# Weight pieces of an mLSTM cell with a gated projection: two blocks at a time, on two DMA queues

## The chip, the core and the metric

The kernel runs on one core of a Trainium2 chip. The core has five engines with an instruction queue each: TensorE (PE in the profile, with its weight loads as PEld), VectorE (DVE), ScalarE (ACT), GpSimd (POOL) and SyncE (SP), which only issues transfers here. Every engine works through its own instructions in the order in which the program wrote them. Sixteen DMA engines move data between HBM and the on-chip memory of 128 partitions; transfers that SP issues stand in the queue that the profile calls q1, those that GpSimd issues in q0. The metric is the device time of one execution in microseconds (us); a kernel's time is the median of several runs.

## The reference

Two parts follow each other. The first is an mLSTM cell over 4 batches, 8 heads, 768 steps and head dimension 40:

```python
m_new = np.maximum(f_gate[:, :, t] + m, i_gate[:, :, t])
f_stab = np.exp(f_gate[:, :, t] + m - m_new)
i_stab = np.exp(i_gate[:, :, t] - m_new)
C = f_stab[:, :, None, None] * C + i_stab[:, :, None, None] * np.einsum('bhd,bhe->bhde', vt, kt)
n = f_stab[:, :, None] * n + i_stab[:, :, None] * kt
h_tilde = np.einsum('bhde,bhe->bhd', C, qt)
denom = np.maximum(np.abs(np.einsum('bhd,bhd->bh', n, qt)[:, :, None]), 1.0)
y[:, :, t] = o * h_tilde / denom          # o: sigmoid of o_gate
```

Its result, as 3072 tokens of 320 features, goes through a gated projection:

```python
g = x @ w_gate                            # 320 x 1536
silu = g * (1.0 / (1.0 + np.exp(-g)))
val = x @ w_val                           # 320 x 1536
return (silu * val @ w_out).astype(np.float32)   # 1536 x 320
```

The three weight matrices are float64 in HBM; all else is float32.

## The kernel before

The 768 steps are cut into 6 groups of 128 (two chunks of 64 each). A group goes through the cell as matrix products (scores of q and k, weighted by a table w_sb, plus what comes from the state C), is turned into xT, and then through the projection. The first group is done in a special way while inputs and weights are still on their way; from the second on all weights lie on the chip, and the projection uses a scheme with fewer products (`gated`, `project_seven`). The order of work is written out by hand, since the kernel asks for a manual schedule.

**Weights in pieces.** The 1536 columns of w_gate and w_val make 12 blocks of 128 columns; a block's gate half goes to partitions 0 to 63 and its value half to partitions 64 to 127, 320 KB each as float64. w_out makes three pieces of four blocks over all 128 partitions. `PIECES` (L162) lists the transfers: before the change blocks 0 to 5 as pieces 0 to 5 of one block, blocks 6 to 11 as pieces 6 to 8 of two blocks, w_out as pieces 9 to 11. `piece_load(p, home, parts)` (L166) issues one piece: a gate transfer (part 0) and two value transfers (parts 1 and 2, the first with four fifths of the bytes). Gate halves go by SP and value halves by GpSimd, except that pieces 2 to 5 go by GpSimd altogether (L200). The raw words land in one of two rotating buffers of the pool tile `raw`, in the tail of h_sb (blocks 2 and 3, a place in which q and k of the first group lie densely before), or in wo_sb (piece 7).

**Conversion.** A block is turned to float32 in four steps: `scale` (L221) with two ScalarE instructions (top, L226, and low, L228), `join` (L231) with two VectorE instructions (L235, L236), and `rounded` (L240) with one addition on GpSimd, or on VectorE for some blocks (L243). There is one top buffer and two low buffers, so blocks are converted one after the other.

**The first group's loop.** `hidden(0, m)` (L740) runs for m = 0 to 11. TensorE multiplies block m (20 matmuls, L748); then the loop converts an older block that `ahead` (L1011) names (block 3 at m = 1, block 4 at m = 2, to block 11 at m = 9); then ScalarE applies silu (L753) and VectorE multiplies (L754) to fill h_sb. So the conversion's instructions stand ahead of the silu on ScalarE, and of the product on VectorE. Two blocks' products fit into the four PSUM banks, so block m + 2 waits for block m's silu and product. Behind each block `slots[m]` (L1012) puts other work:

- 0: pieces 6 and 7 are asked for. 1: `late_sums`, a scan on VectorE. 2: `late_maxima`, the store of M_sb to DRAM by GpSimd, and the load of k for the next group by SP.
- 3: `late_decay`, then on SP the load of w_sb (M_sb read back, spread over partitions), of q and of v.
- 4: an exp, some small tables, and piece 8 (blocks 10 and 11). 5: transposes and decays. 6: transposes of k, `weights_cap` (L530, VectorE on w_sb), piece 9.
- 7: `weights_sub` (L519, VectorE), `weights_exp` (L537, ScalarE), `weigh_values` (L395, GpSimd, with v).
- 8: a memset of q_sb, the scores (L384), piece 10, the load of o_gate. Before these, in the middle of block 8's matmuls, q is transposed (L351) and copied to qT by ScalarE.

After the loop, `project_all` multiplies with w_out, and the groups 1 to 5 follow.

**Ahead of the loop** (L642 to L708) stands the first group's cell work. There SP gets the gates of pieces 0 and 1, GpSimd their values, and then, behind `first_gate(1, ...)` (L692), GpSimd gets pieces 2 to 5 (L693).

SP's and GpSimd's transfers each stand in the order of issue, and an engine that issues can be held at a transfer: SP when the queue is behind, GpSimd when the eighth transfer before has not landed.

Of the kernel before, what the change touches and what calls it, by code (L numbers as in the profile page):

```python
# [12 lines left out]
U32 = mybir.dt.uint32  # L13
AF = mybir.ActivationFunctionType
# [10 lines left out]
def kernel(  # L25
# [18 lines left out]
    nc = tc.nc  # L44
# [9 lines left out]
    NFC = DF // 128  # L54
# [3 lines left out]
    NKC = DM // HP  # L58
    UH = BH // 2
    UA = UH // 2  # L60
    NH = NFC + 1
# [15 lines left out]
    def bank(name, tag="cell"):  # L77
        return psum.tile([128, 512], F32, name=name, tag=tag)
# [41 lines left out]
    wo_sb = const.tile([128, NFC, DM], F32)  # L120
    h_sb = const.tile([128, NH, TW], F32)
# [37 lines left out]


    raws = {}
    PIECES = [("gv", m, 1) for m in range(NFC // 2)] + [("gv", m, 2) for m in range(NFC // 2, NFC, 2)] + [("o", m, 4) for m in range(0, NFC, 4)]  # L162

    homes = {}

    def piece_load(p, home=None, parts=(0, 1, 2)):  # L166
        kind, m, n = PIECES[p]
        if kind == "gv":
            a, d = NKC, n * 128
            gate_w, val_w = (w[:, m * 128:(m + n) * 128].rearrange("(c p) f -> p c f", p=HP) for w in (moe_w_gate, moe_w_val))  # L170
            src = [(slice(0, HP), slice(0, NKC), gate_w), (slice(HP, 128), slice(0, NKC - 1), val_w[:, 1:]),
                   (slice(HP, 128), slice(NKC - 1, NKC), val_w[:, 0:1])]
        else:
            a, d = n, DM
            src = [(slice(0, 128), slice(0, n), moe_w_out[m * 128:(m + n) * 128].rearrange("(a p) d -> p a d", p=128))]
        if src[0][2].dtype == F32:
            for r, cs, w in [src[x] for x in parts if x < len(src)]:
                if kind == "o":
                    nc.sync.dma_start(out=wo_sb[r, m:m + n, :], in_=w)
                else:  # L180
                    for x in range(n):
                        nc.sync.dma_start(out=wgv_sb[r, m + x, cs], in_=w[:, :, ts(x, 128)])
            return
        if p in homes:
            raw = homes[p]
        else:
            if p < 6:
                if p in (0, 4):
                    homes["raw"] = conv.tile([128, 4 * NKC * 128], U32, name="raw")
                base = h_sb[:, NH - NKC:].rearrange("p m t -> p (m t)").bitcast(U32) if p in (2, 3) else homes["raw"]  # L190
                raw = base[:, ds(2 * a * d if p in (1, 3, 5) else 0, 2 * a * d)]
            elif home is None:
                raw = conv.tile([128, 4 * NKC * 128], U32, name="raw")
            else:
                raw = home.rearrange("p a t -> p (a t)").bitcast(U32)
            raw = homes[p] = raw[:, 0:2 * a * d]
        for x in parts:
            if x < len(src):
                r, cs, w = src[x]
                eng = nc.gpsimd if x or 1 < p < 6 else nc.sync  # L200
                eng.dma_start(out=raw[r].rearrange("p (a d) -> p a d", a=a)[:, cs], in_=w.bitcast(U32))
        words = raw.rearrange("p (a d two) -> p a d two", two=2, a=a)
        raws[p] = (words[:, :, :, 0], words[:, :, :, 1])
        split(p)
# [16 lines left out]
    def scale(j):  # L221
        if j in blocks:
            lo, hi, dst = blocks[j]
            a, d = hi.shape[1], hi.shape[2]
            top = conv.tile([128, NKC * 128], F32, name="top", bufs=1).rearrange("p (a d) -> p a d", a=a)
            nc.scalar.mul(top, hi.bitcast(F32), 2.0 ** -112)  # L226
            low = conv.tile([128, NKC * 128], I32, name="low").rearrange("p (a d) -> p a d", a=a)
            nc.scalar.mul(low, lo, 2.0 ** -29)  # L228
            blocks[j] = (low, top.bitcast(U32), dst)
# [81 lines left out]
    step1 = keep1  # L311
# [250 lines left out]
    A, V, G = nc.scalar, nc.vector, nc.gpsimd  # L562
# [63 lines left out]
    def first_gate(P, engs, pad):  # L626
        for u, eng in zip((2 * P, 2 * P + 1), engs):
            x = x_sb[:, u, 0:DM].rearrange("p (h d) -> p h d", d=D)
            eng.tensor_tensor(x, x, o_sb[:, u * H:(u + 1) * H], op=ALU.mult)
        copy(pad, x_sb[:, 2 * P:2 * P + 2, DM:], x_sb[:, 2 * P:2 * P + 2, 0:HP])  # L630
# [12 lines left out]
        copy(eng, state(2)[:, P * UA:(P + 1) * UA], ps)  # L643

    GATE, VALUE = (0,), (1, 2)
    burn(7, "gen")
    for f in (first_mask, first_inputs, first_maxima):
        for x in range(B):
# [19 lines left out]
    for p in range(2):  # L668
        piece_load(p, parts=GATE)
    turn_one(1, q_sb, qT, (V, A))  # L670
    first_values(0)
    piece_load(0, parts=VALUE)
    first_own(0)
    turn_one(1, k_sb, kT, (A, A))
# [15 lines left out]
    first_x(3)  # L690
    seam(0, 0, (A, A, A, A))
    first_gate(1, (G, V), V)  # L692
    for p in range(2, 6):  # L693
        piece_load(p)
    scale(0)
    ps0 = first_state(0, "gen")
    seam(0, 1, (V, A, A, A))
# [312 lines left out]
    on_vector = (9, 10, 11)  # L1010
    ahead = {0: [], 1: [3], 2: [4], 3: [5], 4: [6], 5: [7], 6: [8], 7: [9], 8: [10], 9: [11], 10: [], 11: []}  # L1011
    slots = {  # L1012
        0: [run(piece_load, 6), run(piece_load, 7, wo_sb)],
        1: [run(late_sums)],
        2: [run(late_maxima), run(M_store, G), run(load_all, k_sb, k, 1)],
        3: [run(late_decay), run(weights_load, 1), run(load_all, q_sb, q, 1), run(load_all, v_sb, v, 1)],
        4: [run(nc.scalar.activation, step1, step1, AF.Exp), run(decay_rows), run(cap_table), run(piece_load, 8)],
        5: [run(late_turns), run(decay)],
        6: [run(turn_one, P, k_sb, kT, (A, A)) for P in range(2)] + [run(weights_cap, 0), run(weights_cap, 1), run(piece_load, 9)],
        7: [run(weights_sub, 1, 0), run(weights_sub, 1, 1), run(weights_exp, 0), run(weights_exp, 1), run(weigh_values, G, 0),  # L1020
            run(weigh_values, G, 1)],
        8: [run(nc.gpsimd.memset, q_sb, 0.0), run(do_scores), run(piece_load, 10), run(load_all, o_sb, o_gate, 1)],
        9: [run(do_weigh, 0), run(do_weigh, 1), run(do_decayed, 2)],
        10: [run(do_add, 1, (0,)), run(rounded, 12), run(load_squares, q_sq, q, 2, (0,))],
        11: [run(do_intra, 0), run(do_inter, 1, 0), run(do_gather, 1, 0, False), run(piece_load, 11),
             run(load_squares, q_sq, q, 2, (1,))],
    }
    amid = {8: [run(turn_one, P, q_sb, qT, (A, A)) for P in range(2)], 11: [run(do_add, 1, (1,)), run(do_state, 2)]}
# [122 lines left out]
```

## Time and profile before

| | |
|---|---|
| Median of 3 runs | 516.66 us (516.08 to 516.69) |
| The profiled execution, its own time | 515.42 us |
| Its span, first to last instruction | 513.5 us |
| PE busy, PEld busy | 98%, 83% of the span |
| DVE, ACT, POOL busy | 65%, 41%, 52% |
| Granted TensorE clock | 1.00 |
| HBM read, written | 35.68 MB, 4.01 MB |
| DMA queue q1 (SP) | 36.95 MB, 45.4% of 16 engines |
| DMA queue q0 (GpSimd) | 5.33 MB, 4.7% of 16 engines |

A group of instructions is shown with its line, engine, operation and tiles (out<-in); times are from the start of the span. A timeline row has the start, the length, the engine, the line, the operation, the tiles and the count, and in square brackets the engine's idle time before it with what ended it. SP's rows show how long SP was held at an issue. The DMA share of a stage is the mean busy share of the 16 engines; it can be above 1 where packets overlap. A matmul's end is modelled, so busy PE is not PE at its peak.

### The profile page before, as it was taken

How to read it: one execution, taken by the hardware profiler on the slowest of the kernel's cores; microseconds unless marked ns; L12 is line 12 of the kernel's file. 1: busy time of each engine (PE TensorE's matmuls, PEld its weight loads, DVE VectorE, ACT ScalarE, POOL GpSimd, SP SyncE). 2: the span in 40 equal slices, each digit the busy share in tenths (PEclk: the TensorE clock that was granted, in tenths of full speed). 3: DMA queues.
4: the chain of work that ended last, by engine and by line, in shares of the span. 5: the costliest groups of instructions: out<-in, count | busy, mean ns of one | idle time of the engine just before them, and what ended most of it. 6: DMA issues, size and time to landing. Idle time of an engine off the chain costs nothing.

```text
span 513.5 us, 15092 instructions
## 1 busy us (share of the span) xinstructions
PE 502.5 (98%) x6437; PEld 424.9 (83%) x6437; DVE 332.7 (65%) x543; ACT 208.1 (41%) x404; POOL 264.6 (52%) x296
## 2 busy tenths in 40 slices
PE   8999979999899999999999999999999999999996
PEld 4855545667788899888899888899988899988896
DVE  5889557688897777588467578558558554233421
ACT  3684746448343339321338321338321340223200
POOL 3773442366689663367652357651447650166710
PEclk9999999999999999999999999999999999999999
DMA  9999997798621992501992501992101200000001
GB/s 148 189 213 223 182 180 211 154 156 103 96 46 28 166 124 39 91 4 26 163 129 39 88 8 20 165 130 40 42 3 17 39 2 27 27 1 0 1 14 38
DMA packets 184154, 43.29 MB, mean 84 GB/s; under 512 B 173048, under 2 KB 179592, under 8 KB 183448
## 3 DMA queue, kind: packets, MB, share of 16 engines
q1 hardware_dynamic: 182276, 36.95, 45.4%
q0 software_dynamic: 1680, 5.33, 4.7%
q8 instruction: 50, 0.82, 0.7%
q14 instruction: 16, 0.13, 0.1%
q10 hardware_dynamic: 132, 0.07, 0.0%
HBM read 35.68 MB, written 4.01 MB: 77 GB/s over the span
## 4 chain that ended last, share of the span: by engine, by line
PE 84%; DMA 4%; ACT 4%; DVE 3%; POOL 2%; issue 1%; SPq 1%; DVEq 0%; POOLq 0%
PE gv_x L898 24%; PE o_ps L819 22%; PE gv_y L898 20%; PE gv_ps L748 5%; PE o_ps L765 3%; PE inter L433 2%; DMA w_sb<-M_dram 2%; PE intra L442 2%; PE sp L384 2%; ACT w_sb L534 2%; DMA M_dram<-M_sb 1%; PE add L410 1%; ACT h_sb L583 1%; SPq L368 1%; PE sp L600 1%
## 5 line engine op out<-in xcount | busy, mean ns | idle before, releaser
L898 PE MATMUL gv_x<-xT,wgv_sb 64*128 64x256 f32 x720 | 89.1, 377 | 0.0
L898 PEld LDWEIGHTS gv_x<-xT,wgv_sb 64*128 64x128 f32 x720 | 69.3, 187 | 8.1 <-issue 0.2
L819 PE MATMUL o_ps<-wo_sb,h_sb 128*128 128x160 f32 x480 | 67.4, 300 | 0.0
L819 PEld LDWEIGHTS o_ps<-wo_sb,h_sb 128*128 128x128 f32 x480 | 65.6, 190 | 1.7 <-issue 1.7
L946 ACT ACTIVATE h_sb<-gv_x 128x256 f32<-128x256 f32 x30 | 11.5, 383 | 115.7 <-PE gv_x L898 115.7
L748 PE MATMUL gv_ps<-xT,wgv_sb 64*128 64x512 f32 x240 | 54.3, 596 | 0.1
L748 PEld LDWEIGHTS gv_ps<-xT,wgv_sb 64*128 64x128 f32 x240 | 25.4, 187 | 23.9 <-issue 20.2
L898 PE MATMUL gv_y<-xT,wgv_sb 64*128 64x256 f32 x360 | 43.9, 376 | 0.0
L898 PE MATMUL gv_y<-q_sb,wgv_sb 64*128 64x256 f32 x360 | 43.9, 376 | 0.0
L395 POOL TENSOR_TENSOR vw_sb<-v_sb,w_sb 128x656 f32<-128x656 f32 x10 | 13.8, 1376 | 52.3 <-ACT w_sb L534 40.5
L898 PEld LDWEIGHTS gv_y<-xT,wgv_sb 64*128 64x128 f32 x360 | 34.9, 187 | 4.0
L898 PEld LDWEIGHTS gv_y<-q_sb,wgv_sb 64*128 64x128 f32 x360 | 34.9, 187 | 4.0
L819 PE MATMUL o_ps<-wT,S 128*128 128x160 f32 x240 | 33.4, 299 | 0.0
L819 PEld LDWEIGHTS o_ps<-wT,S 128*128 128x128 f32 x240 | 32.9, 190 | 0.0
L898 PE MATMUL gv_x<-q_sb,sw 64*128 64x256 f32 x240 | 31.0, 377 | 1.2 <-POOL sw L872 1.2
L534 ACT ACTIVATE w_sb<-w_sb,g_T 128x64 f32<-128x64 f32 x128 | 31.0, 334 | 0.0
L919 POOL TENSOR_TENSOR h_sb<-x_sb 128x512 f32<-128x512 f32 x12 | 15.8, 1313 | 24.6 <-ACT x_sb L918 24.6
L939 POOL TENSOR_TENSOR tmp<-tmp 128x512 f32<-128x512 f32 x15 | 20.2, 1344 | 14.9 <-DVE tmp L938 14.9
L919 POOL TENSOR_TENSOR h_sb<-tmp 128x512 f32<-128x512 f32 x13 | 16.5, 1271 | 21.5 <-ACT tmp L918 21.5
L786 POOL TENSOR_TENSOR S<-h_sb 128x256 f32<-128x256 f32 x30 | 22.7, 756 | 9.4 <-DVE h_sb L919 7.4
L765 PE MATMUL o_ps<-wo_sb,h_sb 128*128 128x320 f32 x96 | 27.2, 438 | 0.0
L898 PE MATMUL gv_y<-q_sb,sw 64*128 64x256 f32 x200 | 27.0, 388 | 0.2 <-DVE tmp L916 0.2
(226 smaller groups left out, 988.3 us busy)
## 6 DMA issues: line engine op xcount, KB each, us to landing
w_sb<-M_dram SPq DMA_DIRECT2D x10, 512.0 KB, 6.7
v_sb<-in_v_dram SPq DMA_DIRECT2D x12, 320.0 KB, 5.8
o_sb<-in_o_gate_dram SPq DMA_DIRECT2D x12, 320.0 KB, 5.6
raw<-in_moe_w_out_dram SPq DMA_DIRECT2D x3, 1280.0 KB, 6.8
k_sb<-in_k_dram SPq DMA_DIRECT2D x10, 320.0 KB, 7.7
x_sq<-k_sb SPq DMA_DIRECT2D x64, 40.0 KB, 3.0
q_sb<-in_q_dram SPq DMA_DIRECT2D x32, 64.0 KB, 3.3
out_dram<-tmp SPq DMA_DIRECT2D x24, 80.0 KB, 1.7
```

Source lines behind the costliest of these rows:

```text
L384: nc.tensor.matmul(sp[two][half(i), a, :], lhsT=kT[feats(two), P * UA + a, half(i)], rhs=qT[feats(two), P * UA + a, half(i)], start=True, ...
L395: eng.tensor_tensor(vw_sb[:, heads(P)], v_sb[:, heads(P)], w_sb[:, heads(P), last].to_broadcast([128, UH, D1]), op=ALU.mult)
L433: nc.tensor.matmul(inter[two][half(i), a, :], lhsT=qT[feats(two), P * UA + a, half(i)], rhs=state(2 * n + i)[feats(two), P * UA + a, :], s ...
L534: nc.scalar.activation(w_sb[:, h], w_sb[:, h], AF.Exp, bias=g_T[:, n, h:h + 1], scale=-1.0)
L748: nc.tensor.matmul(ps[i], lhsT=wgv_sb[half(i), m, kc, :], rhs=x[half(i), kc, :], start=(kc == 0), stop=(kc == NKC - 1))
L765: nc.tensor.matmul(ps[u], lhsT=hid(g, m)[:, ts(u, L)], rhs=wo_sb[:, m, :], start=(m == 0), stop=(m == NFC - 1))
L786: eng.tensor_tensor(S1[:, k], lo[:, second_half], hi[:, second_half], op=ALU.add)
L819: nc.tensor.matmul(node[x][:, i], lhsT=lhs(k)[:, ts(i, L)], rhs=rhs(k), start=start and k == 0 and i == 0, stop=stop and k == KH - 1, skip ...
L898: nc.tensor.matmul(ps[:, i, cols], lhsT=lhs(c)[half(i)], rhs=rhs(c)[half(i)], start=start and c == 0, stop=stop and c == n - 1, skip_group ...
L919: (nc.vector if k == KH - 1 else nc.gpsimd).tensor_tensor(h_sb[:, 2 * k + 1], uw[:, 0], uw[:, 1], op=ALU.mult)
L939: nc.gpsimd.tensor_tensor(uw[:, :, second_half], uw[:, :, second_half], uw[:, :, first_half], op=ALU.add)
L946: nc.scalar.activation(h[:, first_half], x[:, 0, first_half], AF.Silu)
```

## The change

Blocks 2 to 9 are listed as pieces of two blocks, so the list has 10 pieces instead of 12 and the later ones get new numbers: 2 (blocks 2 and 3), 3 (4 and 5), 4 (6 and 7), 5 (8 and 9), 6 (10 and 11), 7 to 9 (w_out). Every gate half now goes by SP and every value half by GpSimd. Piece 2 takes the whole tail of h_sb; a one-column memset by GpSimd (`raw_h`) stands in front of it, for which its transfers wait. Piece 3 takes the second `raw` buffer; the others land where the same blocks landed before. Pieces 2 and 3 are asked for where pieces 2 to 5 were. Piece 6 (blocks 10 and 11) is asked for in slot 5 instead of slot 4, and the load of v moves from slot 3 to slot 5, behind it. On SP the order becomes w_sb, q, gates of blocks 10 and 11, v; it was w_sb, q, v, gates of blocks 10 and 11. Nothing is computed in another way.

```diff
-    PIECES = [("gv", m, 1) for m in range(NFC // 2)] + [("gv", m, 2) for m in range(NFC // 2, NFC, 2)] + [("o", m, 4) for m in range(0, NFC, 4)]
+    PIECES = [("gv", 0, 1), ("gv", 1, 1)] + [("gv", m, 2) for m in range(2, NFC, 2)] + [("o", m, 4) for m in range(0, NFC, 4)]
...
-            if p < 6:
-                if p in (0, 4):
+            if p < 2:
+                if p == 0:
                     homes["raw"] = conv.tile([128, 4 * NKC * 128], U32, name="raw")
-                base = h_sb[:, NH - NKC:].rearrange("p m t -> p (m t)").bitcast(U32) if p in (2, 3) else homes["raw"]
-                raw = base[:, ds(2 * a * d if p in (1, 3, 5) else 0, 2 * a * d)]
+                raw = homes["raw"][:, ds(2 * p * a * d, 2 * a * d)]
...
-                eng = nc.gpsimd if x or 1 < p < 6 else nc.sync
+                eng = nc.gpsimd if x else nc.sync
...
+    raw_h = h_sb[:, NH - NKC:]
...
-    for p in range(2, 6):
-        piece_load(p)
+    nc.gpsimd.memset(raw_h[:, 0, 0:1], 0.0)
+    piece_load(2, raw_h)
+    piece_load(3)
...
-        0: [run(piece_load, 6), run(piece_load, 7, wo_sb)],
+        0: [run(piece_load, 4), run(piece_load, 5, wo_sb)],
...
-        3: [run(late_decay), run(weights_load, 1), run(load_all, q_sb, q, 1), run(load_all, v_sb, v, 1)],
-        4: [run(nc.scalar.activation, step1, step1, AF.Exp), run(decay_rows), run(cap_table), run(piece_load, 8)],
-        5: [run(late_turns), run(decay)],
+        3: [run(late_decay), run(weights_load, 1), run(load_all, q_sb, q, 1)],
+        4: [run(nc.scalar.activation, step1, step1, AF.Exp), run(decay_rows), run(cap_table)],
+        5: [run(piece_load, 6), run(load_all, v_sb, v, 1), run(late_turns), run(decay)],
```

In slots 6, 8 and 11 only the numbers of the w_out pieces change (9, 10, 11 to 7, 8, 9).

More of the change, by code (lines that the diff above doesn't have):

```diff
@@ L1012 @@
     slots = {
-        0: [run(piece_load, 6), run(piece_load, 7, wo_sb)],
+        0: [run(piece_load, 4), run(piece_load, 5, wo_sb)],
         1: [run(late_sums)],
         2: [run(late_maxima), run(M_store, G), run(load_all, k_sb, k, 1)],
-        3: [run(late_decay), run(weights_load, 1), run(load_all, q_sb, q, 1), run(load_all, v_sb, v, 1)],
-        4: [run(nc.scalar.activation, step1, step1, AF.Exp), run(decay_rows), run(cap_table), run(piece_load, 8)],
-        5: [run(late_turns), run(decay)],
-        6: [run(turn_one, P, k_sb, kT, (A, A)) for P in range(2)] + [run(weights_cap, 0), run(weights_cap, 1), run(piece_load, 9)],
+        3: [run(late_decay), run(weights_load, 1), run(load_all, q_sb, q, 1)],
+        4: [run(nc.scalar.activation, step1, step1, AF.Exp), run(decay_rows), run(cap_table)],
+        5: [run(piece_load, 6), run(load_all, v_sb, v, 1), run(late_turns), run(decay)],
+        6: [run(turn_one, P, k_sb, kT, (A, A)) for P in range(2)] + [run(weights_cap, 0), run(weights_cap, 1), run(piece_load, 7)],
         7: [run(weights_sub, 1, 0), run(weights_sub, 1, 1), run(weights_exp, 0), run(weights_exp, 1), run(weigh_values, G, 0),
             run(weigh_values, G, 1)],
-        8: [run(nc.gpsimd.memset, q_sb, 0.0), run(do_scores), run(piece_load, 10), run(load_all, o_sb, o_gate, 1)],
+        8: [run(nc.gpsimd.memset, q_sb, 0.0), run(do_scores), run(piece_load, 8), run(load_all, o_sb, o_gate, 1)],
         9: [run(do_weigh, 0), run(do_weigh, 1), run(do_decayed, 2)],
         10: [run(do_add, 1, (0,)), run(rounded, 12), run(load_squares, q_sq, q, 2, (0,))],
-        11: [run(do_intra, 0), run(do_inter, 1, 0), run(do_gather, 1, 0, False), run(piece_load, 11),
+        11: [run(do_intra, 0), run(do_inter, 1, 0), run(do_gather, 1, 0, False), run(piece_load, 9),
              run(load_squares, q_sq, q, 2, (1,))],
```

## The prediction

> **What bounds the kernel now.** I read the page first. TensorE's row is full, and a busy row may hide stalls, so I looked for the stretch in which the change works. The weight blocks come in the first 95 us, behind them the span is made of products that only follow in order. There I asked first for the DMA engines by stage (columns: stage and its length in us; busy time of PE, weight loads, DVE, ACT, POOL; granted clock, DMA share, GB/s):
>
> ```profile
> 26.00:33.00 7.00, 6.94 (x62) 3.94 (x60) 5.72 (x12) 6.55 (x13) 5.18 (x9) 1.00 1.04 218
> 37.00:41.00 4.00, 4.00 (x22) 2.14 (x20) 3.96 (x3) 1.84 (x3) 2.56 (x3) 1.00 1.04 200
> 41.00:44.00 3.00, 3.00 (x18) 1.56 (x16) 2.96 (x6) 0.23 (x1) 1.43 (x2) 1.00 1.05 300
> ...
> 84.00:86.00 2.00, 2.00 (x57) 1.00 (x54) 2.00 (x5) 0.60 (x1) 0.00 (x0) 1.00 1.03 412
> ```
>
> The DMA engines are busy throughout and yet move 218, 200, 300 or 412 GB/s. At 26 to 33 us all is GpSimd's queue, which brings one half of a block at a time to 64 partitions; at 84 to 86 us an output piece goes to 128 partitions; at 41 to 44 us SP brings gate halves (partitions 0 to 63) while GpSimd brings value halves (64 to 127). The queues of that last stretch:
>
> ```profile
> q0 software_dynamic: 167, 0.55, 62.6%
> q1 hardware_dynamic: 167, 0.33, 39.7%
> ```
>
> So GpSimd's queue moved 183 GB/s and SP's 110 beside each other. Next, who waits for weights on ScalarE, whose scaling (L226, L228) is the first of the conversion's steps:
>
> ```profile
> 31.01 0.80 ACT L226 ACTIVATE top<-h_sb 128x640 f32<-128x640 f32 x1 [0.39 <-DMA h_sb<-in_moe_w_val_dram]
> ...
> 34.12 0.80 ACT L226 ACTIVATE top<-h_sb 128x640 f32<-128x640 f32 x1 [1.15 <-DMA h_sb<-in_moe_w_val_dram]
> ...
> 37.17 0.80 ACT L226 ACTIVATE top<-raw 128x640 f32<-128x640 f32 x1 [0.23 <-DMA raw<-in_moe_w_val_dram]
> ...
> 44.51 0.79 ACT L226 ACTIVATE top<-raw 128x640 f32<-128x640 f32 x1 [3.27 <-DMA raw<-in_moe_w_val_dram]
> ...
> 48.72 0.79 ACT L226 ACTIVATE top<-raw 128x640 f32<-128x640 f32 x1 [2.25 <-DMA raw<-in_moe_w_val_dram]
> ```
>
> Blocks 2 to 6 arrive just in time or late for ScalarE. Did TensorE pay? Its timeline:
>
> ```profile
> 27.39 26.12 PE L748 MATMUL gv_ps<-xT,wgv_sb 64*128 64x512 f32 x120
> 53.44 0.80 PE L719 MATMUL tp_g<-x_sq 32*128 32x32 f32 x10
> ...
> 67.64 0.71 PE L351 MATMUL tp_kq<-x_sq,q_sb 64*128 64x64 f32 x16 [0.64 <-DMA q_sb<-in_q_dram]
> 69.98 0.71 PE L351 MATMUL tp_kq<-x_sq,q_sb 64*128 64x64 f32 x16 [1.63 <-DMA q_sb<-in_q_dram]
> ...
> 73.51 2.13 PE L384 MATMUL sp<-qT,kT 40*64 40x64 f32 x126 [0.16 <-ACT qT L143]
> ```
>
> Six blocks take 26.12 us, 4.35 each, and weight loads 0.43 apart make 4.3: hardly. The stall is later: q, then the scores, which wait for ScalarE's copies of qT. What holds these is on VectorE and SP:
>
> ```profile
> 63.95 2.36 DVE L530 TENSOR_TENSOR w_sb<-w_sb,cap 128x1024 f32<-128x1024 f32 x2 [3.52 <-DMA w_sb<-M_dram]
> ```
>
> ```profile
> 32.07 18.12 SPq L139 DMA_DIRECT2D k_sb<-in_k_dram  x1
> ```
>
> ```profile
> 53.42 1.13 SPq L515 DMA_DIRECT2D w_sb<-M_dram  x2
> 54.65 8.65 SPq L139 DMA_DIRECT2D q_sb<-in_q_dram  x2
> 63.40 5.97 SPq L139 DMA_DIRECT2D v_sb<-in_v_dram  x2
> 69.60 1.44 SPq L201 DMA_DIRECT2D raw<-in_moe_w_gate_dram  x1
> ```
>
> SP sat 18.12 us on the second half of k behind the backlog of weights. The chain of waits runs through M_sb's store (issued 46.17, 7.23 us) and w_sb's load (53.96, 9.87 us). Blocks 10 and 11 are asked for at 69.60 and wanted by ScalarE at 76.61.
>
> **The change, part by part.** *Issues.* GpSimd loses the 12 issues of blocks 2 to 5 (0.72, 0.63 and 0.56 us a block, 7.6 us) and gains 4 (2.4 us) and a memset of one column (0.15 by the nearest memset row). It also waited four times there, 2.8 us, for older DMAs. Its next work, the addition for block 3, starts at 37.57 and is needed at 40.4, so this is worth nothing. SP gains two issues of 0.60; it is idle from 22.0 to 30.0, so they are free. They wait for the memset (about 24.0, GpSimd's gating ends at 23.89). Behind them stand the gates of blocks 6 to 9 (which wait for block 1's scaling until 29.97 as before) and k, not wanted until 58.9. Blocks 10 and 11's values (1.17 us of GpSimd, 53.50) move behind the addition for block 7, into 2.33 us idle before that for block 8: free.
>
> *When blocks 2 and 3 are there.* This is the step that can cost. Before, each block was complete by itself: block 2 at 31.0, block 3 at 34.1. Now both come at once, in 640 KB of gate and 640 KB of value. The values need 0.655 MB / 183 GB/s = 3.6 us, the gates 0.655 / 110 = 6.0 us. From an issue at 24.1 and 0.9 us to the first packet they end at 31.0; landing follows some 2.1 us after, as an estimate from block 2 (0.655 MB at 218 behind what is left of block 1 ends near 28.8; there at 30.9). That is 33.1. Bounds: 31.5 when both queues share evenly at 300 GB/s (1.31 MB in 4.4 us), 37 when there is no overlap and blocks 4 and 5 mix in. I take 33.1, from the only stretch with gate and value side by side.
>
> *What 2.1 us later cost.* ScalarE's scaling of block 2 stands ahead of the silu of block 0, and VectorE follows: join, addition, product of block 0, join of block 3, product of block 1, then the scan of late_sums (37.58). VectorE's slack there is the 0.67 us that it waited for the silu of block 1; TensorE's is 1.2 (product of block 0 ends at 34.94, block 2's matmuls begin at 36.15). So 1.5 us passes on to late_sums, the join of block 4, M_sb and TensorE's blocks 4 and 5. Cost 1.5. Block 4 has 2.5 us of slack (37.17 against its join at 41.26, behind the scan), block 5 now comes with it; the waits of 3.27 and 2.25 go, and uncover only ScalarE's idle time.
>
> *What is gained behind it.* Blocks 2 to 9 are 5.24 MB. Two queues side by side (300 GB/s while values last, 200 for the gates left) end near 44.5 instead of 48.4, so k ends near 48.5 and M_sb's store, issued at 47.7, has the engines nearly to itself: landing at 51 (a small load took 2.3). Blocks 10 and 11's values no longer lie beside w_sb's load, whose median to landing is 6.7: w_sb at 57.7 where it was 63.9. VectorE wants it after the product of block 6, 59.75 + 0.69 + 1.3 = 61.7, so its idle 3.52 goes: gain 3.5. q, behind w_sb, lands by 65 even beside the moved values; TensorE wants it at 67.7: its idle 0.64 and 1.63 go, which lie inside the 3.5. What is late next is ScalarE: table load, exp (2.19) and qT copies, at 70.7 where they were at 72.40. All of that is 3.5 - 1.5 = 2.0. Then the gates of blocks 10 and 11, now in front of v: there by 69, wanted at 73. TensorE waited 0.75 where 0.24 is usual for block 8's silu, held by that scaling: gain 0.5. v, moved behind, lands near 71.5 as before; its user on GpSimd waits there already, and the products it feeds are at 83. SP's later issues wait for block 11's scaling, which moves forward too.
>
> Sum: -1.5 + 3.5 + 0.5 = 2.5 us less; beyond 95 us the order is unchanged and TensorE passes a shift on to the end. The profiled execution has a span of 513.5 and a time of 515.42, 1.24 under the median 516.66; taken off the median: **514.2 us**. Each us that block 2 comes later than 33.1 costs about 1.15 (VectorE's whole delay, and what TensorE had left); the gain is 0 at 35.3, and 1.03 lost (0.2%, about what a measurement can tell from no change) at 36.2.
>
> A rule that speaks against it: the Trainium skill, "SBUF — State Buffer", section "Can I just issue two DMAs to hit both halves?", says no: two DMAs on the two halves of the partitions gained 6% and serialize. By it the 218 GB/s would become 231 (an estimate from that page), blocks 2 and 3 with what goes between them would come at 35.6 to 38.4, and the sum would be 0.4 to 3.6 us lost, 517.0 to 520.2. The trace doesn't agree: the row at 41 to 44 us has 300, 38% more than 218.
>
> **Rivals.** *One: no price.* The queues share evenly; block 2 is there at 32.0, 1.3 us less is lost: gain 3.8, 512.9 us. For it: the row at 300. Against: 167 packets of each queue there, and GpSimd's are twice as large.
>
> *Two: SP's gates starve, the kernel gets slower.* Place: the landing of blocks 2 and 3 on ScalarE. In 37 to 41 us the sum was 200, and SP's gates issued at 30.0 took 12.6 us to land. If both halves of blocks 2 to 5 run as at 26 to 33 us, and values of blocks 4 and 5 go ahead of the first gates, 1.96 to 2.62 MB must pass at 218: 25.0 + 9.0 to 12.0 + 2.1 is 36.1 to 39.1. A third of the way, at 37.0, since some overlap is in the rows, the sum is 2.0 lost: 518.6 us. It decides from 36.2 on. Against: both halves of the mix at 37 to 41 went largely to the same partitions, and a GpSimd backlog of four DMAs stood before those gates; now there is one.
>
> *Three: the weights are hidden, nothing moves.* Block 2 at 34.4 to 36.2: the late gain pays the early loss, within 1 us: 516.5. For it: TensorE lost under 1 us to weights before 53 us.
>
> **How the numbers follow.** Forecast (2.5 less, block 2 between 32.3 and 34.4, 513.2 to 515.6): 0.45. Rival one 0.11, rival three 0.20, rival two 0.24. Faster is 0.45 + 0.11 = 0.56, same 0.20, slower 0.24. The range takes in rival one whole (no early loss at all, block 2 at 31.8 or before, is 4.0 less: 512.7) and rival two up to 36.6: 512.5 to 518.2. Left out is the worse half of rival two, 0.12.
>
> **What would show it.** ScalarE's first scaling that reads h_sb begins near 33.1 and the next one 2 to 3 us later with no DMA wait; the DMA rows of 25 to 38 us show near 300 GB/s; SP's 18 us on k end by 47; VectorE's cap (L529 there) has no wait for w_sb; TensorE's transposes of q have none for q; ScalarE's scaling near 72 has none for the gate weights. Wrong makes it: a first scaling after 35, GB/s near 220 with both queues on, or w_sb still waited for.

## The result, and the profile after

The changed kernel took 513.93 us (median of 20 runs, 512.51 to 517.04), the kernel before 516.48 us on the same chips (20 runs, 514.59 to 518.26). The ratio is 0.9959, with a 95% interval from 0.9945 to 0.9974: 2.1 us less (1.3 to 2.8), where 2.5 us were forecast. One of the twelve executions of a kernel further down (single blocks by two queues) and three of the twelve of another (the second with gates before w_sb) took more than 1.5% longer than their kernel's shortest, at a lower granted clock; medians and ratios leave them out. The profiled execution of the changed kernel took 514.3 us, with a span of 511.9.

The total came out near the forecast, in part by luck: the landing on which its largest cost rests was 1.8 us late and the cost larger than its term, and some of what made up for it was not in the sum. I follow the views in the order of the prediction. First the DMA engines by stage, in the changed kernel (columns as before: stage and length, busy time of PE, weight loads, DVE, ACT, POOL, granted clock, DMA share, GB/s):

```profile
26.00:29.00 3.00, 2.94 (x56) 2.21 (x53) 2.75 (x7) 2.97 (x7) 0.93 (x2) 1.00 0.92 206
29.00:32.00 3.00, 3.00 (x16) 1.34 (x12) 2.18 (x4) 2.03 (x5) 1.33 (x3) 1.00 1.02 218
32.00:43.00 11.00, 9.61 (x44) 5.40 (x44) 7.12 (x10) 5.69 (x9) 2.56 (x4) 1.00 1.05 298
```

From 32 us on, gates and values do run beside each other at 298 GB/s. In the six microseconds that decide about blocks 2 and 3 they don't: 206 and 218 GB/s, where GpSimd's halves alone had 218 before. The queues at 26 to 29 us, and then at 29 to 32 us, say why:

```profile
q1 hardware_dynamic: 274, 0.56, 84.0%
q0 software_dynamic: 20, 0.06, 8.5%
...
q0 software_dynamic: 138, 0.52, 81.1%
q1 hardware_dynamic: 75, 0.12, 20.0%
```

First SP's gates had the engines nearly to themselves, and then GpSimd's values. The gates of the first two-block piece, issued at 24.32, landed at 31.03; the values, issued at 24.59 and 25.25, landed at 33.95 and 34.64. So ScalarE's first scaling of that piece begins at 34.86, where I had put 33.1:

```profile
34.86 0.79 ACT L225 ACTIVATE top<-h_sb 128x640 f32<-128x640 f32 x1 [3.83 <-DMA h_sb<-in_moe_w_val_dram]
37.13 0.79 ACT L225 ACTIVATE top<-h_sb 128x640 f32<-128x640 f32 x1 [0.31 <-DVE wgv_sb L235]
```

TensorE pays for it between block 1 and block 2, and its row of blocks, unbroken before, now has a gap. The rest of its timeline in the changed kernel:

```profile
27.76 8.98 PE L749 MATMUL gv_ps<-xT,wgv_sb 64*128 64x512 f32 x40
38.14 17.94 PE L749 MATMUL gv_ps<-xT,wgv_sb 64*128 64x512 f32 x80 [1.40 <-DVE wgv_sb L242]
56.01 0.81 PE L720 MATMUL tp_g<-x_sq 32*128 32x32 f32 x10
...
69.40 1.16 PE L350 MATMUL tp_kq<-x_sq,q_sb 64*128 64x64 f32 x32
72.26 2.58 PE L383 MATMUL sp<-qT,kT 40*64 40x64 f32 x128
74.78 8.98 PE L749 MATMUL gv_ps<-xT,wgv_sb 64*128 64x512 f32 x40
84.45 1.14 PE L409 MATMUL add<-vw_sb,k_sb 64*64 64x41 f32 x62 [0.32 <-DVE w_sb L390]
```

The transposes after block 5 (tp_g) begin at 56.01 where they began at 53.44, 2.57 us later. The scores begin at 72.26, where two of the 128 matmuls began at 73.02 and the rest at 73.51: the loss is regained and about 1 us more. Both waits for q are gone. On VectorE so is the wait of 3.52 for w_sb; what it waits for now, in front of the product of block 6, is ScalarE's silu:

```profile
62.32 0.69 DVE L755 TENSOR_TENSOR h_sb<-tmp,gv_ps 128x512 f32<-128x512 f32 x1 [2.39 <-ACT tmp L754]
62.92 2.35 DVE L529 TENSOR_TENSOR w_sb<-w_sb,cap 128x1024 f32<-128x1024 f32 x2
```

and SP's rows, in the changed kernel, show where w_sb's earlier landing comes from:

```profile
31.74 16.29 SPq L139 DMA_DIRECT2D k_sb<-in_k_dram  x2
52.83 0.49 SPq L514 DMA_DIRECT2D w_sb<-M_dram  x1
```

SP is held on k until 48.03 instead of 50.19, and it asks for w_sb 0.6 us earlier (53.42 before). M_sb's store has GpSimd's queue to itself: at 45 to 50 us only SP's is in use, with k,

```profile
q1 hardware_dynamic: 3134, 0.74, 135.3%
```

where at 46 to 50 us before value halves filled GpSimd's queue (0.55 MB). The store lands 4.23 us after its issue instead of 7.23; but it is issued 2.4 us later (48.59 for 46.17), since VectorE's scan in front of it is late with the blocks. As much again is in w_sb's load: from the issue of its second half it takes 6.8 us instead of 9.9, and lands at 60.14 where it landed at 63.83.

### The profile page after: what moved, and what is told of

It reads as the page before. It is cut to its first block, busy times and chain, and to the rows that moved or that the text cites. A ratio compares the mean times of both kernels' runs of the same rounds, so it can differ in the third digit from the quotient of the medians.

```text
span 511.9 us, 15075 instructions
## 1 busy us (share of the span) xinstructions
PE 502.5 (98%) x6437; PEld 428.4 (84%) x6437; DVE 333.9 (65%) x543; ACT 208.4 (41%) x404; POOL 261.9 (51%) x289
## 4 chain that ended last, share of the span: by engine, by line
PE 85%; ACT 5%; DVE 3%; POOL 2%; issue 2%; DMA 1%; SPq 1%; DVEq 0%; ACTq 0%; POOLq 0%
PE gv_x L899 24%; PE o_ps L820 22%; PE gv_y L899 20%; PE gv_ps L749 6%; PE o_ps L766 3%; PE inter L432 2%; PE intra L441 2%; ACT w_sb L533 2%; PE add L409 1%; PE sp L383 1%; SPq L367 1%; DMA h_sb<-in_moe_w_val_dram 1%; ACT h_sb L582 1%; DVE wgv_sb L235 1%; PE burn L545 1%
## 5 line engine op out<-in xcount | busy, mean ns | idle before, releaser
L749 PEld LDWEIGHTS gv_ps<-xT,wgv_sb 64*128 64x128 f32 x240 | 28.2, 187 | 22.5 <-issue 15.2
```

Of the source, the lines that this page charges most:

```text
L749: nc.tensor.matmul(ps[i], lhsT=wgv_sb[half(i), m, kc, :], rhs=x[half(i), kc, :], start=(kc == 0), stop=(kc == NKC - 1))
```

## The experiments

For each kernel I give the median, and the ratio to the kernel before as it ran beside it on the same chip (517.55 us for the first four, 517.32 for the next four, 517.37 for the next two, 517.34 for the last two), with its 95% interval. The table puts the profiled executions on one clock: times in us from the first projection matmul of the loop, which is each event's start or landing minus the start of the first gv_ps matmul (27.39 before, 27.76 after, 28.0 to 28.5 in the others). "Block 2" and "block 6" are the starts of these blocks' matmuls, and "w_sb's cap" is the start of VectorE's instructions on it.

| | block 2 | block 6 | w_sb landed | w_sb's cap | q landed | scores | end |
|---|---|---|---|---|---|---|---|
| before | 8.8 | 27.1 | 36.4 | 36.6 | 42.5 | 45.6 | 486.1 |
| changed | 10.4 | 29.3 | 32.4 | 35.2 | 41.8 | 44.5 | 484.1 |
| pieces only (e1) | 10.1 | 29.1 | 32.6 | 34.9 | 41.8 | 44.3 | 485.4 |
| move only (e2) | 8.8 | 27.4 | 33.6 | 33.7 | 43.7 | 48.4 | 486.3 |
| blocks 2, 3 as before (e11) | 8.7 | 27.1 | 31.4 | 33.0 | 39.5 | 42.3 | 481.7 |
| v by GpSimd (e12) | 10.0 | 28.9 | 31.9 | 34.8 | 46.2 | 50.9 | 488.8 |

The profiled execution of the move alone was the longest of its six (516.12 us; the other five 513.2 to 514.2), so its row from q on may not be its usual course: it holds a wait of 3.41 us for q, told below. The move's second trace was the longest of its seven as well (517.05 us; the others 511.5 to 513.8) and has the same wait (3.59), so no trace shows this kernel in one of its usual executions.

**The two parts of the change, each alone.** First the pieces without the move. Edit to the changed kernel:

```diff
-        3: [run(late_decay), run(weights_load, 1), run(load_all, q_sb, q, 1)],
-        4: [run(nc.scalar.activation, step1, step1, AF.Exp), run(decay_rows), run(cap_table)],
-        5: [run(piece_load, 6), run(load_all, v_sb, v, 1), run(late_turns), run(decay)],
+        3: [run(late_decay), run(weights_load, 1), run(load_all, q_sb, q, 1), run(load_all, v_sb, v, 1)],
+        4: [run(nc.scalar.activation, step1, step1, AF.Exp), run(decay_rows), run(cap_table), run(piece_load, 6)],
+        5: [run(late_turns), run(decay)],
```

> The changed kernel with the two-block pieces on two queues, but blocks 10 and 11 and v asked for where they were before (slots 4 and 3). Theory 'the move gives': the late part of the gain (w_sb no longer waited for) comes from taking blocks 10 and 11's values off w_sb's load, and the pieces alone only cost the lateness of block 2: no faster than before, 516 to 518 us, w_sb waited for again. Theory 'the overlap gives' (the prediction's): gate and value side by side free the DMA engines sooner, so most of the gain is here: 514 to 515 us, block 10's wait of 0.5 us back, w_sb not waited for.

Measured: 515.88 us, 0.9969 (0.9954 to 0.9983), 1.6 us less than before. VectorE didn't wait for w_sb, and TensorE's wait in front of block 10 was back (0.70 us), as the second theory said. But here v and the values of blocks 10 and 11 were also asked for at other moments than before: the values at 57.24, 3.1 us behind the issue of w_sb's second half, where before they were asked for at 53.50, in front of it. So this run doesn't tell the overlap from the later values.

Then the move without the pieces. Edit to the kernel before:

```diff
-        3: [run(late_decay), run(weights_load, 1), run(load_all, q_sb, q, 1), run(load_all, v_sb, v, 1)],
-        4: [run(nc.scalar.activation, step1, step1, AF.Exp), run(decay_rows), run(cap_table), run(piece_load, 8)],
-        5: [run(late_turns), run(decay)],
+        3: [run(late_decay), run(weights_load, 1), run(load_all, q_sb, q, 1)],
+        4: [run(nc.scalar.activation, step1, step1, AF.Exp), run(decay_rows), run(cap_table)],
+        5: [run(piece_load, 8), run(load_all, v_sb, v, 1), run(late_turns), run(decay)],
```

> The kernel before with one-block pieces, and only the move of blocks 10 and 11 in front of v and into slot 5. 'The move gives': block 2 is there at 31 us as before, w_sb's load has the engines to itself and lands by 61: faster than the changed kernel or equal, 513 to 514.5 us. 'The overlap gives': the backlog of weights still ends at 48 us, w_sb lands at 63 or later, only block 10's wait of 0.5 us goes: 516 us.

Measured: 513.96 us, 0.9930 (0.9910 to 0.9950), 3.6 us less than before, and again, with the changed kernel beside it:

> The kernel before with the move of blocks 10 and 11 and v alone, again, beside the changed kernel. If the two-block pieces cost what the lateness of block 2 shows (TensorE 2.2 us behind at 54 us) it is 1 to 2 us faster than the changed kernel; if that loss is taken up later by the wait for q, both are the same within 0.7 us.

513.63 us, 0.9929 (0.9903 to 0.9956): 1.0 us less than the changed kernel beside it, which had

> The changed kernel itself, beside the others on one chip: 0.9959 of the kernel before, as known.

514.56 us, 0.9948 (0.9928 to 0.9969). The difference of the two lies within their intervals. The parts gain 1.6 and 3.6 us alone and 2.1 to 2.7 together, so they are not to be added. The table has the reason: each of them alone brings w_sb by 32.6 to 33.6, in time for VectorE, so the second one finds that wait gone. In the move alone VectorE's row reads

```profile
61.73 2.38 DVE L530 TENSOR_TENSOR w_sb<-w_sb,cap 128x1024 f32<-128x1024 f32 x2 [0.39 <-DMA w_sb<-M_dram]
```

without anything done about the weights in front of it. The load of w_sb took 7.1 us from its second issue to landing in the move alone (54.54 to 61.60), where it took 9.87 before. The values of blocks 10 and 11 are asked for 3.3 us behind that issue there, and not in front of it.

**What the late blocks 2 and 3 cost.** Three kernels bear on it. In the first, blocks 2 to 5 are single blocks as before, with the gate by SP and the value by GpSimd, and the move is kept. Edit to the move alone:

```diff
-                eng = nc.gpsimd if x or 1 < p < 6 else nc.sync
+                eng = nc.gpsimd if x else nc.sync
```

> The move as in the changed kernel, blocks 2 to 5 as one-block pieces, but gate halves by SP and value halves by GpSimd. The halves of block 2 are half as large, so it should be complete by 31 to 32 us and no early time be lost, while the queues overlap later as in the changed kernel: 512 to 513 us by both theories. Rival, the queues take turns transfer by transfer and block 2's values wait for the gates of blocks 3 to 5: block 2 at 34 or later and 514 us or more.

Measured: 515.89 us, 0.9969 (0.9944 to 0.9994), a miss. SP's gates for four blocks, asked for at 20.25 to 22.26, went ahead of GpSimd's value for block 1, asked for at 22.36, and TensorE stopped one block earlier, as the rival in the expectation had it, but by block 1 instead of block 2:

```profile
35.47 23.17 PE L748 MATMUL gv_ps<-xT,wgv_sb 64*128 64x512 f32 x100 [2.87 <-DVE wgv_sb L243]
```

It is the same turn-taking that made block 2 late in the changed kernel: in both traces what SP had asked for went first.

The second takes the wait away: the changed kernel, but the scaling of blocks 2 and 3 reads words of v_sb that have long been there, so the conversion of those two blocks doesn't wait for what was loaded and doesn't use it; everything else is done.

```diff
+            if j in (2, 3):
+                other = v_sb.rearrange("p h d -> p (h d)").bitcast(U32)[:, 0:2 * NKC * 128]
+                other = other.rearrange("p (a d two) -> p a d two", two=2, a=NKC)
+                lo, hi = other[:, :, :, 0], other[:, :, :, 1]
```

> The changed kernel, with blocks 2 and 3 converted from the words of v_sb, which is there since 16 us, instead of from piece 2; all transfers stay. The weights of blocks 2 and 3 are thereby wrong, and the time of waiting for piece 2 is left out. If the lateness of block 2 is what the change costs, the kernel is 1.5 to 2.5 us faster than the changed one, 511.5 to 512.5; if later waits (w_sb, q) take its place, it gains under 0.7 us.

Measured: 512.34 us, 0.9892 (0.9873 to 0.9911), against 0.9948 and 0.9959 for the changed kernel itself: 2.9 or 3.5 us, more than the 1.5 to 2.5 expected.

The third does it with the right weights: blocks 2 and 3 come one after the other by GpSimd as before, blocks 4 and 5 are a two-block piece by both queues, and all that follows is the changed kernel's. Edit to the changed kernel (in the slots only the later pieces' numbers change, which isn't shown):

```diff
-    PIECES = [("gv", 0, 1), ("gv", 1, 1)] + [("gv", m, 2) for m in range(2, NFC, 2)] + [("o", m, 4) for m in range(0, NFC, 4)]
+    PIECES = [("gv", m, 1) for m in range(4)] + [("gv", m, 2) for m in range(4, NFC, 2)] + [("o", m, 4) for m in range(0, NFC, 4)]
...
-                eng = nc.gpsimd if x else nc.sync
+                eng = nc.gpsimd if x or p in (2, 3) else nc.sync
...
-    nc.gpsimd.memset(raw_h[:, 0, 0:1], 0.0)
-    piece_load(2, raw_h)
+    piece_load(2)
     piece_load(3)
+    homes[4] = conv.tile([128, 4 * NKC * 128], U32, name="raw")
+    nc.gpsimd.memset(homes[4].bitcast(F32)[:, 0:1], 0.0)
+    piece_load(4)
```

> The changed kernel, but blocks 2 and 3 come one after the other by GpSimd as before (complete at 31 and 34 instead of together at 34.9); blocks 4 and 5 are a two-block piece whose gates wait for a memset behind these; the move of blocks 10, 11 and v as in the change. If the late blocks 2 and 3 are what keeps the change behind the move alone: as the move alone, 0.992 to 0.994 of before, some 513.6, with TensorE's first six blocks unbroken. If that lateness is absorbed further on (q's second half lands at a fixed time): as the changed kernel, 0.995 to 0.997, 514.5 to 515.8, with the time back as a wait for q at 66 to 72 us.

Measured: 512.91 us, 0.9914 (0.9889 to 0.9940), 4.4 us less than before and the shortest time of the kernels that compute the whole. TensorE's timeline:

```profile
28.17 26.11 PE L752 MATMUL gv_ps<-xT,wgv_sb 64*128 64x512 f32 x120
...
67.61 1.16 PE L351 MATMUL tp_kq<-x_sq,q_sb 64*128 64x64 f32 x32
...
70.47 2.58 PE L384 MATMUL sp<-qT,kT 40*64 40x64 f32 x128
```

The six blocks are unbroken again and no wait for q is left. Against the changed kernel block 6, the scores and the end all come 2.2 to 2.4 us earlier in the table: what block 2's lateness costs there stays to the end and is not absorbed. And against the move alone (0.9930), M_sb's store lands at 24.2 instead of 26.0 from the loop's start and w_sb at 31.4 instead of 33.6: that is the overlap of the later pieces, without its price at the start. (q lands at 39.5 instead of 43.7, but that is beside the move's long execution.) In the total the two differ by 0.8 us, within their intervals, so a gain of this kernel over the move alone is not shown.

**The order around v and the gates of blocks 10 and 11.** Four kernels change this alone. Values of blocks 10 and 11 one slot later, edit to the move alone:

```diff
-        5: [run(piece_load, 8), run(load_all, v_sb, v, 1), run(late_turns), run(decay)],
+        5: [run(piece_load, 8, None, GATE), run(load_all, v_sb, v, 1), run(late_turns), run(decay)],
...
+        6: [run(piece_load, 8, None, VALUE)] + [run(turn_one, P, k_sb, kT, (A, A)) for P in range(2)] + [run(weights_cap, 0), run(weights_cap, 1), run(piece_load, 9)],
```

> As the move alone, but blocks 10 and 11's values are asked for in slot 6, behind GpSimd's addition for block 8 (about 60.5 us) instead of 57.9. In the move alone and in the changed kernel these values go between q's first and second half and q's second half lands at 69.6 to 71.5. If that is the wait that is left, q is complete by 67.5 and the kernel is 1 to 2 us faster than the move alone; rival, the values come too late for block 10 (wanted near 71) or ScalarE's exp and copies hold the scores anyway: within 0.7 us of it.

Measured: 515.81 us, 0.9969 (0.9952 to 0.9986), 2 us lost against the move alone, which neither of the two expectations had. By the traces the wait moved from q (3.41 to 1.40) to block 10: ScalarE's scaling of block 10 waited 3.56 us until 75.38, and TensorE stopped 1.96 us, until 80.58, in front of that block's matmuls.

v in front of the gates, edit to the changed kernel:

```diff
-        5: [run(piece_load, 6), run(load_all, v_sb, v, 1), run(late_turns), run(decay)],
+        5: [run(load_all, v_sb, v, 1), run(piece_load, 6), run(late_turns), run(decay)],
```

> The changed kernel with v asked for before the gates of blocks 10 and 11, all else as it is. In the changed kernel v lands at 75.8, and GpSimd's weighting, memset and decays then lie beside VectorE's conversion of blocks 10 and 11, whose instructions take 1.8 and 1.7 us instead of 0.82. If that costs, VectorE's rows are short again and the kernel gains 0.3 to 0.8 us, less the 0.5 us for block 10's gates, which come later: 0.3 faster to 0.3 slower. Rival, asking for the gates before v is what gives the gain at the end: 0.5 to 1 us slower than the changed kernel.

Measured: 516.30 us, 0.9982 (0.9967 to 0.9998), 1.2 to 1.8 us slower than the changed kernel (by its two ratios), more than either expectation had. By the traces, where it is 1.25 us, none of that is there yet behind the first product of the weighted values (the loop's time is 57.5 us in this kernel and 57.8 in the changed one). It arises inside the second:

```profile
90.09 0.43 PE L409 MATMUL add<-vw_sb,k_sb 64*64 64x41 f32 x12 [0.96 <-issue]
```

The same wait with "issue" as its reason (0.68 us), at the same matmul, is in the kernel before and in the pieces alone, and in no other kernel. The trace names no releaser, but it has the transfers of the instruction queue (q8 in the profile), 16 KB each. In these three kernels one starts 2.1 to 2.3 us before that matmul would else begin (87.81 before, 88.51, and 87.06 here), and the wait ends 2.8 to 3.0 us behind that start. In the other eleven traces it starts 2.9 to 5.0 us before the matmul, and there is no wait. So TensorE very probably waited for its next instructions; no run tests that alone, and why this transfer starts later in three kernels stays open. The order of v and the gates is not shown to be worth anything else.

The gates in front of w_sb and q, edits to the changed kernel and to the kernel of the third experiment on blocks 2 and 3 (there with piece 7):

```diff
-        3: [run(late_decay), run(weights_load, 1), run(load_all, q_sb, q, 1)],
+        3: [run(late_decay), run(piece_load, 6, None, GATE), run(weights_load, 1), run(load_all, q_sb, q, 1), run(load_all, v_sb, v, 1)],
-        5: [run(piece_load, 6), run(load_all, v_sb, v, 1), run(late_turns), run(decay)],
+        5: [run(piece_load, 6, None, VALUE), run(late_turns), run(decay)],
```

> The changed kernel, with the gates of blocks 10 and 11 in front of w_sb's load on SP (the DMA engines stand idle there for near 2 us until M_sb's store has landed), their values in slot 5 as in the change, and v right behind q as it was before. If v behind the gates is what slows VectorE in the changed kernel, and gates behind v are what cost when v goes first, this has neither: VectorE's rows short, no wait for block 10, w_sb landing about 1.3 us later but still in time: 0.5 to 1.5 us faster than the changed kernel (0.992 to 0.994 of the kernel before). Rival: w_sb and q, now later, hold TensorE: equal or slower (0.995 or more).

> As the run with the gates in front of w_sb, and blocks 2 and 3 as one-block pieces by GpSimd as before the change, with blocks 4 and 5's gates held until GpSimd has asked for these. Block 2 is then at ScalarE near 31 us, and TensorE loses nothing before 40 us. If the early lateness costs what the run without the wait for blocks 2 and 3 showed, it is 1 to 2.5 us faster than the run with the gates in front of w_sb alone; if block 3 comes late instead, or q holds TensorE anyway, within 0.7 us.

Measured: 515.32 us, 0.9966 (0.9950 to 0.9983), and 514.76 us, 0.9957 (0.9939 to 0.9974). Neither gained on the changed kernel, and the second was 0.5 us ahead of the first, within the 0.7 of its second case. The first one's trace, of its longest execution (517.28 us), has no wait for q; block 2 came later still there (scaling at 36.21, a stop of 2.34 us), so it doesn't say why this kernel didn't gain. The second stands 0.9957 to 0.9914 against the same kernel with the gates behind q, 2.2 us slower. w_sb landed 3.3 us later there (34.7 for 31.4) and q 3.2 (42.7 for 39.5), and TensorE waited for q again:

```profile
68.86 0.71 PE L351 MATMUL tp_kq<-x_sq,q_sb 64*128 64x64 f32 x16 [1.23 <-DMA q_sb<-in_q_dram]
70.88 1.12 PE L351 MATMUL tp_kq<-x_sq,q_sb 64*128 64x64 f32 x16 [1.31 <-DMA q_sb<-in_q_dram]
```

**v asked for by GpSimd.** Edit to the changed kernel:

```diff
-        5: [run(piece_load, 6), run(load_all, v_sb, v, 1), run(late_turns), run(decay)],
+        5: [run(piece_load, 6), run(load_all, v_sb, v, 1, G), run(late_turns), run(decay)],
```

> The changed kernel, but GpSimd asks for v itself, right behind the values of blocks 10 and 11 (about 60 us), where it is idle, instead of SP behind the gates. If late v, and so GpSimd's weighting of it beside VectorE's conversion of blocks 10 and 11, is what slows VectorE (1.81 and 1.71 us for 0.82): v lands near 70, the weighting follows the exponential at 71 to 74, the conversion's instructions take 0.8 to 0.9 again, TensorE's wait for the product on w_sb goes, 513.0 to 514.0 (0.992 to 0.995 of before). If the slow rows have another reason, they stay and the time is the changed kernel's. If v, asked for earlier, takes bandwidth from q or the values, a wait for q of 1 us or more appears at 66 to 72 us and nothing is gained: 514.5 to 516.

Measured: 518.83 us, 1.0031 (1.0011 to 1.0051), 3.7 to 4.3 us slower than the changed kernel (by its two ratios), more than I had allowed for. v landed at 70.54 and 74.01, and VectorE's conversion is quick again (below), but q's second half landed at 74.33 instead of 69.57:

```profile
74.46 1.11 PE L350 MATMUL tp_kq<-x_sq,q_sb 64*128 64x64 f32 x16 [4.43 <-DMA q_sb<-in_q_dram]
```

In SP's queue v had stood behind q; on the other queue it ran beside q and delayed it.

## Why the prediction was right, point by point

- *Issues are free.* Held. SP issued the gates of blocks 2 to 5 at 24.32 and 24.97 (24.1 forecast); the values of blocks 10 and 11 took GpSimd 1.35 us at 58.40, in front of an addition that then waited for VectorE (0.34).
- *Blocks 2 and 3 at 33.1 us.* Failed: 34.86, inside the bounds (31.5 to 37) but outside the 32.3 to 34.4 of the forecast, on the side that I called rival two, and 0.14 us short of the 35 that I had named as a sign of being wrong. The DMA rows of 25 to 38 us, to be near 300 GB/s, showed it only from 32 on. The step took the two queues' rates of 41 to 44 us (183 and 110 GB/s beside each other) for the first six microseconds too. There 1.31 MB passed at 206 to 218 GB/s, one queue after the other, and from about 26.0 instead of 25.0, since block 1 still came at 24 to 26 us. 1.31 MB / 215 is 6.1; 26.0 + 6.1 is 32.1, and the landing at 34.64 followed 2.5 us behind (2.1 had been taken). The row of 26 to 33 us in the old profile, GpSimd's halves alone, was the better one for this term. The rule on two DMAs of the Trainium skill, "SBUF — State Buffer", section "Can I just issue two DMAs to hit both halves?", which the prediction weighed, describes this start and not the stretch after it, 298 GB/s; and its outcome, slower by 0.4 to 3.6, did not come.
- *Cost 1.5 us, and 1.15 for each us later.* By this 34.86 costs 1.5 + 1.15 * 1.76 = 3.5. The third experiment on these blocks puts it at 2.2 to 2.4 by the trace and 1.8 to 2.3 by the ratios (0.9914 against 0.9948 and 0.9959); taking the wait away gave 2.9 or 3.5. By the traces, then, the term was 0.7 to 0.9 us too small, since the landing was late; by the ratios, 0.3 to 2.0, with wide intervals. The slope was rather too steep: by it the gain left at 34.86 would have been 0.5 us, outside the measured 1.3 to 2.8.
- *w_sb in time, gain 3.5; q in time inside it.* Right in kind, not in its landings. SP was held on k until 48.03 (47 forecast). M_sb's store was issued at 48.59 (47.7) and landed at 52.82 (51), w_sb at 60.14 (57.7); VectorE wanted it at 62.92. q's second half landed at 69.57 (65 forecast) where TensorE began with the first half at 69.40: no margin was left, and the two traces of the move alone, with its later w_sb, missed it by 3.41 and 3.59 us. In the repeat of the changed kernel, its longest execution (516.09 us), TensorE waited 0.34. I had given the gain to overlap and move as one chain; the move is enough for w_sb by itself, and so are the pieces with the values asked for later that came with them.
- *Scores.* qT's copies at 71.61 (70.7 forecast, 72.40 before).
- *Gates of blocks 10 and 11 before v, gain 0.5.* Right for the wait that it was about: the 40 matmuls with the wait for block 8's silu took 9.77 us before, 9.51 with v first and 8.98 in the changed kernel. TensorE gave 0.32 of that back waiting for w_sb's product. By the traces, what v first loses in all (1.2 to 1.8 us by the ratios) is the wait at 90 us, of which the sum knew nothing. *v lands at 71.5 as before*: it landed at 75.79 (73.0 before), and GpSimd's weighting with it, into VectorE's conversion.
- *Sum.* Forecast -1.5 + 4.0 = 2.5. In the profiled executions, counted from the loop's first matmul, block 6 is 2.2 us later; the matmuls behind the first product of weighted values are 1.2 earlier (57.8 for 59.0), so 3.4 were gained; those behind the second are 2.2 earlier (61.6 for 63.8), where the wait with "issue" fell away, another 1.0 by these starts; the end is 2.0 earlier. (This is one execution of each.) So -2.2 + 3.4 + 1.0 stands in place of -1.5 + 4.0, with 0.2 lost again later: the mechanism was right, but its two terms together came to 1.2 instead of 2.5, and the rest came from a wait that the sum didn't have. That the total was near is luck to that extent. Where blocks 2 and 3 come as before, the late gain at the same point is 4.3, near the 4.0.
- *Smaller readings.* "GpSimd's are twice as large" is 1.7 times (0.55 for 0.33 MB, 167 packets each). For queues that share evenly the text gives a landing of 31.5 and one of 32.0. ScalarE wanted blocks 10 and 11 from 74.43 on; at 76.61 it had waited 2.18 us for them. None of these carries the total.

Of the rivals, one fell with the turns at the start. Three's condition came true (block 2 between 34.4 and 36.2); its outcome, within 1 us of no change, did not, since the early loss is 2.2 to 2.4 us by the traces, where its slope said 3.5, and the wait at 90 us fell away. Two's mechanism was there, halves that don't overlap, but it stopped short of 36.2, where it decides.

## What to carry to other kernels

Where two transfers of one need go by two queues, the need is met by the later one, and at the start of a burst the queues may take turns, as they did here: put the first, urgent pieces on one queue as small as they are wanted, and the wide two-queue pieces behind them. Two edits that remove the same wait don't add up; test each alone: here the smaller edit alone gave 3.6 us where both gave 2.1 to 2.7, though the intervals overlap. In a full queue, order the loads by when their users would stop the critical engine, and look for who shares the engines when one of them moves.

## What the runs showed of the hardware

*VectorE beside GpSimd.* When v comes late, GpSimd weighs it while VectorE converts blocks 10 and 11. In the kernel with blocks 2 and 3 as before the rows can be read one against the other. VectorE's timeline:

```profile
73.10 0.83 DVE L236 SCALAR_TENSOR_TENSOR wgv_sb<-top,wgv_sb 128x640 uint32<-128x640 uint32 x1
74.06 1.71 DVE L243 CUSTOM_DVE_ANT_0 wgv_sb<-wgv_sb,low 128x1280 uint16<-128x1280 uint16 x1
...
76.80 1.80 DVE L236 SCALAR_TENSOR_TENSOR wgv_sb<-top,wgv_sb 128x640 uint32<-128x640 uint32 x1
78.75 0.83 DVE L243 CUSTOM_DVE_ANT_0 wgv_sb<-wgv_sb,low 128x1280 uint16<-128x1280 uint16 x1
```

and GpSimd's:

```profile
73.36 1.73 POOL L395 TENSOR_TENSOR vw_sb<-v_sb,w_sb 128x656 f32<-128x656 f32 x1 [12.97 <-ACT low L228]
76.40 1.53 POOL L395 TENSOR_TENSOR vw_sb<-v_sb,w_sb 128x656 f32<-128x656 f32 x1 [1.31 <-DMA v_sb<-in_v_dram]
```

The same two VectorE instructions take 0.83 us when they start with no weighting under way and 1.71 and 1.80 when they start while a weighting runs; they end 0.68 and 0.67 us behind its end (75.09 and 77.93), so most of their work came behind it. GpSimd's first weighting, which starts while a VectorE instruction runs, takes 1.73. With v by GpSimd, where the weighting fell into VectorE's idle time, it took 1.30, and VectorE's second joins and additions of blocks 10 and 11 took 0.82 each. This agrees with the Trainium skill, "SBUF — State Buffer", section "Who interferes with whom": VectorE instructions with two inputs in SBUF and GpSimd instructions that read SBUF exclude each other, and the second waits until the first has ended. In the changed kernel TensorE's wait of 0.32 us for w_sb's product (1.36 and 0.32 in the repeat) may come of it; no run shows that alone.

*The clock after a wait.* In the profiled executions in which TensorE waited 1.96 us or more for one thing in this stretch, its granted clock fell to half for 3.41 or 6.83 us. In the move alone, after 3.41 us of waiting for q:

```profile
70.40:73.80 3.40, 2.00 (x20) 1.54 (x22) 0.00 (x0) 1.73 (x4) 0.00 (x0) 0.50 1.24 170
73.80:77.20 3.40, 3.40 (x40) 1.41 (x40) 1.44 (x3) 2.60 (x4) 1.01 (x1) 0.50 0.87 151
```

The eight matmuls behind it took 3.76 us instead of 1.96. It also followed 3.59 us (the move again) and 4.43 (v by GpSimd), both for 6.83 us; and, for 3.41 us, the waits of 2.87 (single blocks by two queues), 2.34 (the changed kernel with gates before w_sb), 1.96 (values one slot later) and 1.23 + 1.31 close together (the other kernel with gates before w_sb, from 70.7). It made these waits dearer than their length. It did not follow the waits of 1.40 and 1.43 us of the changed kernel and its repeat, nor the 0.64 and 1.63 close together of the kernel before. The Trainium skill, "TensorE: Matmul & The Clock Gate", section "What's actually happening", gives windows of about 3.4 us by which the clock is halved and restored; the stretches agree, but here waits shorter than a window were enough.
